# Queries' first block and the last block of rows at the matrix engine's full width, with half of x copied

## The chip, the cores and the metric

The kernel runs on one core of a Trainium2 chip. The core has a matrix engine (TensorE; PE in the profile, its weight loads PEld), VectorE (DVE), ScalarE (ACT), GpSimd (POOL) and DMA queues that SyncE (SP) issues. They run side by side, each through its own list of instructions in order, and wait for one another by semaphores. The metric is the device time of one execution in microseconds.

## The reference

Block-causal attention over 576 positions (8 batches, 8 heads, head size 64), and a mixer on its output:

```python
scores = scale * np.matmul(q, k.transpose(0, 1, 3, 2))
scores = np.where(block_i >= block_j, scores, -1e9)      # blocks of 64 positions
attn = softmax(scores)
x = matmul(attn, v)                                       # heads side by side: (8, 576, 512)
theta = x @ w_theta
y = w_tok_r @ (x * cos(theta)) + w_tok_i @ (x * sin(theta))
u = x + y
out = u + maximum(u @ w_ch, 0)
```

## The kernel before

Every product is done in float16 parts: an operand is a high part and a low part, and three matmuls (high by high, low by high, high by low) make one product. Heads come in pairs (`Pair`, 32 of them; head `hh` = 0 or 1 of a pair holds partitions 0 to 63 or 64 to 127 of the q and k tiles). Positions stand in the order 64 to 575 and then 0 to 63, so each head has four tiles of 128 queries, `i` = 3, 2, 1, 0, and a last half tile `i` = 4, which is the first 64 queries.

For one pair these steps run. `q_high`, `k_high` (POOL) and `q_low`, `k_low` (DVE) cut q and k in parts. `scores_wide` and `scores_narrow` multiply them on PE with 64 rows of the array per head, two heads beside each other (lines 552 and 558). `scores_first` (line 580) does the first 64 queries of both heads in quarters of the array, 64 by 64: three products by two heads, six matmuls. `maxima` and `less` (DVE, lines 597 and 602), `exponentials` and `high` (ACT, 607 and 618) and `low` (DVE, 622) make the attention parts, and a DMA transposes them (`turn`). `weighted` (line 645) multiplies them with v on PE, into one bank of PSUM, `o`, that all heads share. Of a head's 15 blocks the last, `i` = 4, holds both heads' first 64 queries; each head takes its 64 columns of the block as weights, and writes them twice, to partitions 0 to 63 and 64 to 127, since the mixer reads the half tile of x from both halves. That is six matmuls with 64 columns of weights behind 42 with 128. `normalise` (DVE) is three instructions: add a small number, take the reciprocal `r`, and multiply `o` by it into `xn` (lines 651, 653 and 657).

The mixer of a batch then turns x (759, 762, 765), multiplies by w_theta (773), takes sines and cosines (780 to 799), multiplies by x on POOL (808), cuts z in parts (817, 822), does the token mix (838, 831), and the channel product (856) with its closing steps (842 to 865).

The order of the work is a table. The kernel lists 3437 steps with what each needs; `ORDER` gives the sequence in which they are emitted, and so the list of each engine, and `BANKS` gives the PSUM banks. Steps of several pairs and batches are interleaved. The first matmuls of a step carry its waits.

Of the kernel before, what the change touches and what calls it, by code (L numbers as in the profile page):

```python
# [14 lines left out]
F16 = mybir.dt.float16  # L15
BF16 = mybir.dt.bfloat16
I32 = mybir.dt.int32
U32 = mybir.dt.uint32
AF = mybir.ActivationFunctionType
ALU = mybir.AluOpType  # L20
# [8 lines left out]
QK_BUFS = 2  # L29
# [208 lines left out]


@with_exitstack  # L240
def attention_phase_mixer(
    ctx: ExitStack,
    tc: tile.TileContext,
    qk: bass.AP,
    v: bass.AP,
    w_theta: bass.AP,
    w_tok: bass.AP,
    w_ch: bass.AP,
    out: bass.AP,
):  # L250
# [857 lines left out]
```

## Time and profile before

| | us |
|---|---|
| median of 3 runs | 728.31 (726.88 to 729.43) |
| profiled execution: span | 723.6 |
| what the median has beyond that span | 4.7 |
| PE busy | 640.6 (89%) |
| DVE busy | 588.8 (81%) |
| ACT busy | 589.0 (81%) |
| POOL busy | 270.9 (37%) |

The shares of busy time are means over stages: a start with the weights' preparation, a long stretch in which attention of one batch runs beside the mixers of others, and an end with mixers alone. A matmul's row gives its latency, and many are under way at once, so the cost of a matmul on PE is read from start to start.

### The profile page before, as it was taken

The numbers are of one execution on the slowest core, as the hardware profiler recorded it, in microseconds if no ns is written. First come the engines' busy times: TensorE is split into PE (matmuls) and PEld (weight loads), VectorE is DVE, ScalarE is ACT, GpSimd is POOL, SyncE is SP. The second block draws the span as 40 slices with busy tenths as digits, with TensorE's granted clock in tenths as the row PEclk, the third lists the DMA queues.
The fourth block names the chain that finished last, engine by engine and source line by source line (L and its number), as shares of the span: only waits on it lengthen the run. The fifth ranks groups of instructions, "written<-read, shape, count | busy, mean of one in ns | idle before, by whom it ended". The sixth has DMA issues, their size and how long they took to land.

```text
span 723.6 us, 19051 instructions
## 1 busy us (share of the span) xinstructions
PE 640.6 (89%) x7899; PEld 462.0 (64%) x7899; DVE 588.8 (81%) x1157; ACT 589.0 (81%) x900; POOL 270.9 (37%) x328
## 2 busy tenths in 40 slices
PE   0236489689999999999999999999999999999997
PEld 0124355566577767776667866777577577867776
DVE  6999999999888877888899879888888889642423
ACT  4899989999899789977999789969998899447231
POOL 3121120765155417441356302760083351412620
PEclk9656689899999999999999999999999999999999
DMA  8899999698768785784889994879879719840001
GB/s 297 306 252 195 204 145 192 172 169 159 141 187 175 141 181 152 150 194 90 178 194 198 176 184 119 176 181 154 185 177 183 144 31 157 168 73 17 34 34 66
DMA packets 263399, 114.54 MB, mean 158 GB/s; under 512 B 250896, under 2 KB 250896, under 8 KB 263312
## 3 DMA queue, kind: packets, MB, share of 16 engines
q1 hardware_dynamic: 263312, 113.33, 72.2%
q8 instruction: 61, 1.00, 0.6%
q14 instruction: 26, 0.21, 0.1%
HBM read 40.96 MB, written 9.44 MB: 70 GB/s over the span
## 4 chain that ended last, share of the span: by engine, by line
PE 52%; DVE 21%; ACT 17%; issue 6%; DMA 3%; POOL 0%; DVEq 0%; ACTq 0%; SPq 0%
PE g L838 13%; PE g L645 7%; PE s L838 7%; PE s L773 5%; DVE m L597 5%; PE g L856 4%; DVE p L622 4%; ACT t L607 4%; PE g L773 4%; PE s L856 4%; PE s L552 3%; ACT p L618 2%; PE g L552 2%; DVE rr L785 1%; DMA w_raw<-in_w_tok 1%
## 5 line engine op out<-in xcount | busy, mean ns | idle before, releaser
L622 DVE SCALAR_TENSOR_TENSOR p<-t,p 128x1600 f16<-128x1600 f32 (+3 forms) x80 | 121.8, 1525 | 18.6 <-ACT p L618 18.3
L838 PEld LDWEIGHTS <-zh 128*128 128x128 f16 x1152 | 112.8, 98 | 31.6 <-issue 0.2
L645 PE MATMUL g<-v,pt 128*128 128x65 f16 (+1 forms) x3072 | 112.1, 198 | 18.5 <-DMA pt<-p 8.3
L645 PEld LDWEIGHTS <-pt 128*128 128x128 f16 (+1 forms) x3072 | 105.7, 101 | 30.5 <-issue 12.0
L838 PE MATMUL g<-wT_h,zl 128*128 128x288 f16 x414 | 118.8, 287 | 1.3 <-DVE zl L822 1.0
L838 PE MATMUL g<-wT_h,zh 128*128 128x288 f16 x414 | 119.2, 288 | 0.5 <-DVE rr L785 0.3
L838 PE MATMUL g<-wT_l,zh 128*128 128x288 f16 x414 | 118.7, 287 | 0.0
L607 ACT ACTIVATE t<-s,m,size 128x576 f32<-128x576 f32 (+1 forms) x128 | 97.8, 777 | 17.7 <-DVE m L602 12.1
L808 POOL TENSOR_TENSOR aa<-aa,xn 128x256 f32<-128x256 f32 (+1 forms) x96 | 79.6, 847 | 63.0 <-ACT aa L797 43.4
L618 ACT ACTIVATE p<-t 128x1600 f16<-128x1600 f32 (+3 forms) x80 | 99.6, 1252 | 1.3 <-DMA pt<-p 0.3
L597 DVE TENSOR_REDUCE m<-s 128x1 f32<-128x576 f32 (+1 forms) x128 | 84.6, 680 | 4.6 <-PE s L558 4.1
L607 ACT ACTIVATE t<-g,m,size 128x320 f32<-128x320 f32 (+2 forms) x160 | 80.5, 532 | 3.9 <-DVE m L602 2.8
L773 PEld LDWEIGHTS <-xT 128*128 128x128 f16 x480 | 46.1, 98 | 51.2 <-issue 0.5
L808 POOL TENSOR_TENSOR rr<-rr,xn 128x256 f32<-128x256 f32 x64 | 59.0, 936 | 46.5 <-ACT rr L799 46.5
L838 PEld LDWEIGHTS <-zl 128*128 128x128 f16 x576 | 56.5, 98 | 19.7 <-issue 2.5
L552 PEld LDWEIGHTS <-qh 64*128 64x128 f16 x896 | 37.0, 98 | 45.0 <-issue 18.4
L597 DVE TENSOR_REDUCE m<-g 128x1 f32<-128x320 f32 (+2 forms) x160 | 56.5, 374 | 4.3 <-PE g L558 2.1
L856 PEld LDWEIGHTS <-wch_h 128*128 128x128 f16 x512 | 47.8, 98 | 17.4 <-issue 3.8
L822 POOL TENSOR_TENSOR zl<-rr,zh 128x512 f16<-128x512 f32 x32 | 41.1, 1287 | 37.7 <-ACT zh L817 31.5
L518 POOL TENSOR_SCALAR qh<-rq,size 128x576 f16<-128x576 f32 x32 | 28.7, 898 | 65.2 <-PE g L558 45.3
L849 DVE SCALAR_TENSOR_TENSOR ul<-u,size_ch,uh 128x576 f16<-128x576 f32 x32 | 28.0, 886 | 26.8 <-ACT uh L845 26.8
L773 PE MATMUL g<-wth_h,xT 128*128 128x512 f16 x160 | 47.6, 379 | 0.1
(152 smaller groups left out, 1552.2 us busy)
## 6 DMA issues: line engine op xcount, KB each, us to landing
rv<-in_v SPq DMA_DIRECT2D x16, 768.0 KB, 5.2
rq<-in_qk SPq DMA_DIRECT2D x16, 576.0 KB, 4.8
rk<-in_qk SPq DMA_DIRECT2D x16, 576.0 KB, 4.8
out<-u SPq DMA_DIRECT2D x32, 288.0 KB, 2.8
w_raw<-in_w_tok SPq DMA_DIRECT2D x9, 576.0 KB, 4.8
w_raw<-in_w_theta SPq DMA_DIRECT2D x4, 512.0 KB, 5.5
w_raw<-in_w_ch SPq DMA_DIRECT2D x4, 512.0 KB, 4.1
pt<-p SPq DMA_TRANSPOSE x80, 5.8
```

What stands on the lines that cost most here:

```text
L518: nc.gpsimd.tensor_scalar(out=self.qh, in0=self.raw("q"), scalar1=self.of.ups[0], scalar2=0.0, op0=ALU.mult, op1=ALU.add)
L552: nc.tensor.matmul(to[hh][:, col:col + n], lhsT=qq[rows, 64 + P * i:64 + P * i + P], rhs=kk[rows, k0:k0 + n], start=nn == 0 and col % 512 ...
L597: nc.vector.tensor_reduce(out=self.m[:, i:i + 1], in_=self.scores_of(i), axis=AX.X, op=ALU.max)
L607: nc.scalar.activation(out=t_parts[self.hh][:, to:to + n], in_=self.scores_of(i), func=AF.Exp, scale=self.pair.of.scale, bias=self.m[:, NI ...
L618: nc.scalar.mul(hi, x, LIFT)
L622: nc.vector.scalar_tensor_tensor(out=lo, in0=x, scalar=LIFT, in1=hi, op0=ALU.mult, op1=ALU.subtract)
L645: nc.tensor.matmul(o[to, i, :], lhsT=pp, rhs=vv[:, slot, hh, :], start=first, stop=last)
L773: nc.tensor.matmul(g, lhsT=xT[:, dt, xx + i, :], rhs=ww[:, dt, :], start=dt == 0 and n == 0, stop=dt == NDT - 1 and n == 2)
L808: nc.gpsimd.tensor_tensor(out=cd, in0=cd, in1=self.xns[dt][:, i0:i0 + ni, :], op=ALU.mult)
L822: engine.tensor_tensor(out=zl, in0=cv, in1=zh, op=ALU.subtract)
L838: nc.tensor.matmul(g, lhsT=zz[:, kk, cols], rhs=ww[:, kk, ts], start=(n == 0 and kk == k0 and nn == 0), stop=False)
L856: nc.tensor.matmul(g[:, 0:HS], lhsT=ww[:, dt, e * P:(e + 1) * P], rhs=uu[:, dt, th * HS:(th + 1) * HS], start=dt == 0 and n == 0, stop=dt ...
```

## The change

`scores_first` becomes three matmuls over the whole array. For that the host lays q out with 64 more columns: the first 128 columns hold the first 64 queries of head 0 (on partitions 0 to 63, zeros below) and then those of head 1 (on partitions 64 to 127, zeros above), so that one matmul with 128 rows gives both heads. The q tiles and their parts are therefore 640 wide instead of 576.

`weighted` treats the last block as the others: three matmuls with 128 columns of weights. The half of `o` that belongs to the other head holds nothing of use for this head, and a new DVE instruction in `normalise` multiplies the right 64 rows of `o` by `r` once more and writes them to the other 64 partitions of `xn`.

`junk`, which only receives the absolute values of a sum on ACT, has one byte an element. `ORDER` and `BANKS` are found anew.

```diff
 ORDER = [
-    24, 25, 26, 27, 28, 29, 0, 173, 8, 177, 16, 1, 2, 3, 174, 9, 4, 10, 32, 11, 178, 12, 56, 185, 17, 186, 33, 18,
...
 BANKS = (
...
-    junk = const.tile([P, PG * NI * P], BF16, name="junk")
+    junk = const.tile([P, PG * NI * P], U8, name="junk")
...
-            return ld.tile([P, S], F16, tag=tag, name=tag, bufs=QK_BUFS)
+            return ld.tile([P, S + D if tag[0] == "q" else S], F16, tag=tag, name=tag, bufs=QK_BUFS)
...
-                            nc.tensor.matmul(to[hh][:, col:col + n], lhsT=qq[rows, 64 + P * i:64 + P * i + P], rhs=kk[rows, k0:k0 + n],
+                            nc.tensor.matmul(to[hh][:, col:col + n], lhsT=qq[rows, P + P * i:P + P * i + P], rhs=kk[rows, k0:k0 + n],
...
         def scores_first(self):
             for nn, qq, kk in self.products():
-                for hh in range(2):
-                    rows = slice(hh * D, hh * D + D)
-                    nc.tensor.matmul(self.first[rows], lhsT=qq[rows, 0:64], rhs=kk[rows, 0:64], start=nn == 0, stop=nn == 2,
-                                     tile_position=(hh * D, hh * D))
+                nc.tensor.matmul(self.first, lhsT=qq[:, 0:P], rhs=kk[:, 0:64], start=nn == 0, stop=nn == 2)
...
-                        pp, rows = source[:, block, :], [slice(0, P)]
-                        if i == 4:
-                            pp, rows = pp[:, 64 * hh:64 * hh + 64], [slice(0, 64), slice(64, P)]
-                        for to in rows:
-                            nc.tensor.matmul(o[to, i, :], lhsT=pp, rhs=vv[:, slot, hh, :], start=first, stop=last)
+                        nc.tensor.matmul(o[:, i, :], lhsT=source[:, block, :], rhs=vv[:, slot, hh, :], start=first, stop=last)
...
                                         in1=self.r.unsqueeze(2).broadcast_to([P, NI, D]), op=ALU.mult)
+                mine, other = (slice(x * D, x * D + D) for x in (hh, 1 - hh))
+                nc.vector.tensor_tensor(out=m.xns[pair.pr][other, NI - 1, mine], in0=o[mine, NI - 1, 0:D],
+                                        in1=self.r[mine, NI - 1:NI].broadcast_to([D, D]), op=ALU.mult)
...
+    q_first = np.zeros((B, G, P, PG, P), q.dtype)
+    for rows in (slice(0, D), slice(D, P)):
+        q_first[:, :, rows, :, rows] = q[:, :, rows, :, 0:D]
```

On PE, the first scores of pair 19 (`qh`, `ql` and `kh`, `kl` are the parts of q and k, `g_112` the bank that `o` and the first scores share) stand between two products of the channel step in both kernels. Before:

```order
L580 LDWEIGHTS qh
L580 MATMUL g_112<-kh,qh 64x64
L580 LDWEIGHTS qh
L580 MATMUL g_112<-kh,qh 64x64
L580 LDWEIGHTS ql
L580 MATMUL g_112<-kh,ql 64x64
L580 LDWEIGHTS ql
L580 MATMUL g_112<-kh,ql 64x64
L580 LDWEIGHTS qh
L580 MATMUL g_112<-kl,qh 64x64
L580 LDWEIGHTS qh
L580 MATMUL g_112<-kl,qh 64x64
```

and now:

```order
L853 MATMUL g_110<-uh,wch_l 128x288
L579 LDWEIGHTS qh
L579 MATMUL g_112<-kh,qh 128x64
L579 LDWEIGHTS ql
L579 MATMUL g_112<-kh,ql 128x64
L579 LDWEIGHTS qh
L579 MATMUL g_112<-kl,qh 128x64
L853 LDWEIGHTS wch_h
```

Six matmuls of a quarter of the array became three of the whole.

The end of a head's weighted sum on PE (head 30; `pt` is the transposed attention, `v` the parts of v, `zh` a part of the mixer's z). Before:

```order
L645 MATMUL g_112<-v_85,pt_104 128x65
L645 LDWEIGHTS pt_104
L645 MATMUL g_112<-v_85,pt_104 64x65
L645 LDWEIGHTS pt_104
L645 MATMUL g_112<-v_85,pt_104 64x65
L645 LDWEIGHTS pt_104
L645 MATMUL g_112<-v_86,pt_104 64x65
L645 LDWEIGHTS pt_104
L645 MATMUL g_112<-v_86,pt_104 64x65
L645 LDWEIGHTS pt_104
L645 MATMUL g_112<-v_85,pt_104 64x65
L838 LDWEIGHTS zh
```

and now:

```order
L639 LDWEIGHTS pt_104
L639 MATMUL g_112<-v_85,pt_104 128x65
L639 LDWEIGHTS pt_104
L639 MATMUL g_112<-v_86,pt_104 128x65
L639 LDWEIGHTS pt_104
L639 MATMUL g_112<-v_85,pt_104 128x65
L835 LDWEIGHTS zh
```

The half-width matmuls are gone, and three at full width close the head.

On DVE, the closing of head 31 with its waits (`r` is the reciprocal, `xn` the x of the pair). Before:

```order
L651 TENSOR_SCALAR r<-g_112 128x5 [waits PE_49]
L653 RECIPROCAL r<-r 128x5 [waits DVE_49]
L657 TENSOR_TENSOR xn<-g_112,r 128x5x64 [waits DVE_49,Activation_49]
L526 SCALAR_TENSOR_TENSOR ql<-rq,size,qh 128x576 [waits Pool_49]
L762 TENSOR_TENSOR xp<-xn,xp 128x640 [waits DMAHW0_49,Activation_49]
```

and now:

```order
L645 TENSOR_SCALAR r<-g_112 128x5 [waits PE_49]
L647 RECIPROCAL r<-r 128x5 [waits DVE_49]
L651 TENSOR_TENSOR xn<-g_112,r 128x5x64 [waits DVE_49]
L654 TENSOR_TENSOR xn<-g_112,r 64x64 [waits DVE_49]
L846 SCALAR_TENSOR_TENSOR ul<-u_4694,size_ch,uh 128x576 [waits Activation_49]
L759 TENSOR_TENSOR xp<-xn,xp 128x640 [waits DMAHW1_49,Activation_49]
```

The new instruction stands behind the multiplication, and waits for it on its own engine; what follows differs by the new table.

## Rows read from the trace of the kernel before

**Rows 1.** The page: the span, and each engine's busy time (share), instructions.
```profile
span 723.6 us, 19051 instructions
PE 640.6 (89%) x7899; PEld 462.0 (64%) x7899; DVE 588.8 (81%) x1157; ACT 589.0 (81%) x900; POOL 270.9 (37%) x328
```

**Rows 2.** Busy time by stage; the header names the columns.
```profile
core 0: us, PE busy (x) PEld busy (x) DVE busy (x) ACT busy (x) POOL busy (x), PEclk, DMA share, GB/s
0.00:165.00 165.00, 93.16 (x1349) 64.29 (x1350) 152.85 (x343) 146.67 (x248) 50.61 (x82) 0.80 0.92 215
165.00:590.00 425.00, 418.52 (x5287) 299.73 (x5286) 369.73 (x699) 377.31 (x552) 179.24 (x202) 1.00 0.77 163
590.00:620.00 30.00, 29.48 (x374) 22.47 (x372) 27.96 (x47) 26.76 (x42) 12.63 (x15) 1.00 0.70 122
620.00:723.60 103.60, 99.42 (x900) 75.54 (x895) 38.22 (x71) 38.21 (x61) 28.43 (x32) 1.00 0.24 61
```

**Rows 3.** DVE's longest waits, 165 to 620 us: total us, times, longest.
```profile
DVE p L622 <- ACT p L618: 16.2, 14, 3.4
DVE rr L785 <- ACT aa L780: 8.4, 11, 1.9
DVE r L651 <- PE g L645: 6.6, 8, 1.9
```

**Rows 4.** PE in order of time, a weighted sum's end: start, us, count.
```profile
332.53 0.41 PE L645 MATMUL g<-v,pt 128*128 128x65 f16 x7
...
332.65 0.28 PE L645 MATMUL g<-v,pt 128*64 128x65 f16 x6
332.87 0.30 PE L838 MATMUL g<-wT_h,zh 128*128 128x288 f16 x1
```

**Rows 5.** The same weighted sum, whole.
```profile
331.30 1.64 PE L645 MATMUL g<-v,pt 128*128 128x65 f16 x48
```

**Rows 6.** PE in order of time, first scores between two channel products.
```profile
370.44 0.29 PE L856 MATMUL g<-ul,wch_h 128*128 128x288 f16 x1
370.56 0.29 PE L856 MATMUL g<-uh,wch_l 128*128 128x288 f16 x1
370.77 0.22 PE L580 MATMUL g<-kh,qh 64*64 64x64 f16 x2
370.83 0.20 PE L580 MATMUL g<-kh,ql 64*64 64x64 f16 x2
370.86 0.20 PE L580 MATMUL g<-kl,qh 64*64 64x64 f16 x2
370.99 0.30 PE L856 MATMUL g<-uh,wch_h 128*128 128x288 f16 x1
```

**Rows 7.** PE in order of time, two ends of the other scores.
```profile
330.40 0.22 PE L558 MATMUL g<-ones,mask_q 64*128 64x128 bf16 x1
330.55 0.30 PE L838 MATMUL g<-wT_h,zh 128*128 128x288 f16 x1
...
350.20 0.22 PE L558 MATMUL s<-ones,mask_q 64*128 64x128 bf16 x2
350.35 0.22 PE L580 MATMUL g<-kh,qh 64*64 64x64 f16 x2
...
350.56 0.30 PE L838 MATMUL g<-wT_h,zh 128*128 128x288 f16 x1
```

**Rows 8.** DVE, ACT and POOL groups by shape: busy us, mean ns, idle before.
```profile
L657 DVE TENSOR_TENSOR xn<-g,r 128x320 f32<-128x320 f32 x64 | 31.1, 486 | 3.1 <-ACT t L607 1.6 <-DVE r L653 0.5
L651 DVE TENSOR_SCALAR r<-g 128x5 f32<-128x5 f32 x64 | 10.0, 157 | 15.8 <-PE g L645 14.1 <-ACT t L607 1.6
L597 DVE TENSOR_REDUCE m<-g 128x1 f32<-128x64 f32 x32 | 6.9, 216 | 2.1 <-ACT t L607 2.0
L822 DVE TENSOR_TENSOR zl<-aa,zh 128x256 f16<-128x256 f32 x16 | 8.3, 517 | 0.3 <-ACT zh L817 0.3
L526 DVE SCALAR_TENSOR_TENSOR ql<-rq,size,qh 128x576 f16<-128x576 f32 x32 | 28.4, 887 | 2.4 <-POOL qh L518 2.4
L737 ACT ACTIVATE junk<-rv 128x1280 bf16<-128x1280 f32 x16 | 20.3, 1269 | 1.4 <-DMA rv<-in_v 1.3
L737 ACT ACTIVATE junk<-rq 128x1152 bf16<-128x1152 f32 x16 | 18.6, 1164 | 0.1
L518 POOL TENSOR_SCALAR qh<-rq,size 128x576 f16<-128x576 f32 x32 | 28.7, 898 | 65.2 <-PE g L558 45.3 <-issue 9.1 <-PE g L580 5.2
```

**Rows 9.** DVE in order of time, a head's closing.
```profile
333.18 0.19 DVE L653 RECIPROCAL r<-r 128x5 f32<-128x5 f32 x1
333.40 0.49 DVE L657 TENSOR_TENSOR xn<-g,r 128x320 f32<-128x320 f32 x1
```

**Rows 10.** Line 552 until 162 us, and PE in order of time behind it.
```profile
L552 PE MATMUL s<-kh,qh x64: 187/290/605, 16.5 to 144.0; 64*128 64x64 f16 x32, 64*128 64x512 f16 x16, 64*128 64x384 f16 x16
...
162.18 0.42 PE L552 MATMUL s<-kh,qh 64*128 64x512 f16 x4
...
590.82 0.42 PE L552 MATMUL s<-kh,qh 64*128 64x512 f16 x4 [0.18 <-ACT t L607]
```

More of the change, by code (lines that the diff above doesn't have):

```diff
@@ L18 @@
 U32 = mybir.dt.uint32
+U8 = mybir.dt.uint8
 AF = mybir.ActivationFunctionType
@@ L34 @@
 ORDER = [
[178 rows of a table removed]
[177 rows of a table added]
 ]
 BANKS = (
-    "6555046500302240123540123640123560123540123540123650123640123540123540123460123540123560123560123460123650123460"
-    "1234601234501234601234601235401235601236401234501236401235401236401235401234501234501236401236454260645665611660"
-    "6425451201054465450410201125045446566640505146450620154064566154055530410416604565165504145605061546650064161165"
-    "405623065434601256253044530560235465102"
+    "5611645600406140123640123450123540123560123450123260123450123540123460123640123560123540123650123450123450123450"
+    "1234601235401236401234601236401236401234601236501236401235601235401236401235401234601235601235465041645646540542"
+    "4644450611056626564606101216046464556601505565643051450055654055155520640654604516565606056426150445541251045065"
+    "416036452636046151143624532652053461502"
 )
@@ L243, in attention_phase_mixer @@
     tc: tile.TileContext,
-    qk: bass.AP,
+    q: bass.AP,
+    k: bass.AP,
     v: bass.AP,
@@ L251, in attention_phase_mixer @@
     nc = tc.nc
-    B, _, NG, P, PG, S = qk.shape
+    B, NG, P, PG, S = k.shape
     D = P // 2
@@ L728, in load @@
             self.scales_of(what, g).make()
-            shape, src = ([P, PG, NV, 2, D], v[self.b, g]) if what == "v" else ([P, PG, S], qk[self.b, "qk".index(what), g])
+            shape, src = ([P, PG, NV, 2, D], v[self.b, g]) if what == "v" else ([P, PG, (S, S + D)[what == "q"]], (k, q)[what == "q"][self.b, g])
             self.raw[what, g] = ld.tile(shape, F32, tag=f"r{what}{g}", name=f"r{what}")
@@ L1083 @@
     v_pad[:, :, :, :, 1:5] = v[..., 64:S, :].reshape(B, G, PG, 2, 4, P, D)
+    q, k = (a.reshape(B, G, PG, 2, S, D).transpose(0, 1, 3, 5, 2, 4).reshape(B, G, P, PG, S) for a in (q, k))
+    q_first = np.zeros((B, G, P, PG, P), q.dtype)
+    for rows in (slice(0, D), slice(D, P)):
+        q_first[:, :, rows, :, rows] = q[:, :, rows, :, 0:D]
     laid = {
-        "qk": np.stack([a.reshape(B, G, PG, 2, S, D).transpose(0, 1, 3, 5, 2, 4).reshape(B, G, P, PG, S) for a in (q, k)], axis=1),
+        "q": np.concatenate([q_first, q[..., D:]], axis=-1),
+        "k": k,
         "v": v_pad.transpose(0, 1, 5, 2, 4, 3, 6),
```

354 rows, old and new, of the table ORDER are left out of this document.

## The prediction

> **What bounds the kernel now.** I read the page's busy times first [rows 1]: PE 640.6 us of 723.6, DVE and ACT 81% each. That mean hides three stages, so the busy times by stretch came next [rows 2]. In the first 165 us DVE is busy 152.85 us and PE only 93.16: this start is bound by DVE, with ACT close by. From 165 to 590 us PE is busy 418.52 of 425 us (98.5%), DVE 87%, ACT 89%: PE bounds, but two engines are near. After 620 us DVE and ACT are under 40% and PE is at 96%. Third, the waits from 165 to 620 us [rows 3]: DVE's longest are for ACT's high part (16.2 us), then for ACT's rounding (8.4) and for the weighted sum (6.6), so DVE's idle time is partly spent in a chain with ACT, not only because PE is late. Last, PE in order of time, start to start, since a matmul's own duration is latency.
>
> **What the change removes on PE.** In a weighted sum the last full-width matmul starts at 332.53, the first of half width at 332.65, and the next step at 332.87 [rows 4]. The 42 full ones start between 331.30 [rows 5] and 332.53, 1.23 us over 41 steps, or 0.03 us each. So the six of half width cost 332.87 - 332.56 = 0.31 us, most of it on going in and coming out. Three of full width cost 3 x 0.03 = 0.09. Saved: 0.22 us a head, 14.1 us for 64 heads.
>
> First scores between two full-width steps: the matmul before them starts at 370.56, a 288-column one takes 0.12 (370.44 to 370.56), so the next could start at 370.68; it starts at 370.99 [rows 6]. The six cost 0.31 us, three at 0.03 cost 0.09 (the nearest row: 65 columns against full weights): 0.22 saved. Behind the other scores the way back to full width costs 0.15 alone (330.40 to 330.55), and with first scores between 0.36 (350.20 to 350.56) [rows 7]: the six cost 0.21, saved 0.12. Between two steps of the other scores, three at full width need their own way in (those 0.15) and a way back to half rows, which I estimate at the 0.09 that the way into quarters takes (0.21 from 370.56 to 370.77, less the 0.12); of the six's 0.36 little is left to save, 0.03. The orders have mostly the first two kinds; I take 0.17, bounds 0.03 and 0.22: 32 x 0.17 = 5.4 us, bounds 1.0 and 7.0.
>
> Only what lies where PE bounds counts. Eight pairs' wide scores (16 matmuls of 512 columns) lie ahead of 162 us, so the group at 162.18 is pair 8's [rows 10], and the start ends there. Ahead of it both orders have 14 closed heads. That leaves 50 heads x 0.22 = 11.0 and 24 pairs x 0.17 = 4.1: **15.1 us off the path** (11.7 to 16.3).
>
> For pricing small tiles the Trainium skill has another rule (TensorE: Matmul & The Clock Gate, part 3 on packing small matmuls): tiles in different rows and columns of the array run concurrently, so two quarter-array matmuls take about the time of one. The trace agrees that they start in pairs [rows 6], but not that the group is as cheap as three full ones: 0.31 us against 0.09. By that rule alone PE would gain nothing, which is the last rival below.
>
> **What it adds on DVE.** 64 new instructions, 64 by 64, PSUM to SBUF. No row has this form. Between 157 ns for 5 columns and 486 for 320 [rows 8] a line gives 219 ns at 64 columns; the reduction over 64 columns out of PSUM takes 216. I take 0.22. Bounds: 0.157, and 0.317 (the row with two tensors out of SBUF, 517 ns at 256 columns, brought to 64 by that line's 1.04 ns a column). The copy waits for the instruction before it, on its own engine. Such a pair is seen at 333.18: 0.19 long, the dependent one starts at 333.40, so 0.03 after the end [rows 9]. Each copy thus costs 0.25 us of DVE (0.19 to 0.35), 16.0 us in all. `ql` grows from 576 to 640 columns: in proportion 887 x 64/576 = 0.10 us [rows 8], 32 times, 3.2 us (from 0, if the 64 columns are free).
>
> The copy also keeps the bank `o` 0.25 us longer. The next head's weighted sum waits for it, and PE holds what stands behind that sum; but from 165 us on some 8.5 us pass per head (425 us for 50), against about 1.6 for a sum [rows 5] and 1.2 for its closing with the copy, so the order has room, and I count nothing; uncovered it would be 50 x 0.25 = 12.5 us.
>
> In the start, DVE bounds: 14 copies and 8 `ql` are 3.5 + 0.8 = **4.3 us on the path** (0 if the new order puts off other DVE work; 7 if steps of later heads come ahead as well).
>
> From 165 to 590 us DVE gets 46 copies and 22 `ql`, 11.5 + 2.2 = 13.7 us, while the stretch should shrink by about 13. It would be busy 383 of 412 us, 93% instead of 87%. What that does to PE no row of this stretch shows. It is 0 if all of DVE's 55 idle us can shrink: from 590 to 620 us DVE is busy 27.96 of 30, also 93%, and PE still 29.48 [rows 2]. It is 13.7 if none can, since each added microsecond then delays the scores' maxima and low parts by which PE is fed. As about half of the waits in rows 3 are on ACT, which is at 89% and gains no speed, I take **4 us**, nearer to the row that shows 93%.
>
> **What lies beside.** ACT's sum over q grows by 128 columns, (1269 - 1164) = 0.105 us, 16 times, 1.7 us; POOL's `qh` by at most 898 x 64/576 = 0.10 us, 32 times, at 37% busy [rows 1, 8]. ACT has 48 us idle in the long stretch, and both are covered there; uncovered ACT's part costs 1.7. The bytes of `junk` are written, not read: nothing. q's DMAs carry a ninth more, 16 times; they are issued a batch ahead, and the DMA engines are at 0.77 of their time [rows 2]. In the start, at 0.92, it may cost up to 1 us, inside the bound above. The new tables keep the makeup: pair, head and mixer steps stand in nearly the same counts ahead of the same places, and I give their reshuffling no gain or loss of its own.
>
> **Sum.** -15.1 + 4.3 + 4 = -6.8 us on the profiled execution: span 716.8. The runs' median is 4.7 us above that span, and the change touches nothing outside it: **721.5 us**.
>
> **Rivals.**
> 1. *Everything added is hidden.* For it: DVE has 55 idle us in the long stretch and the table was found with the copy in it. Against it: DVE's 12 idle us in the start are short waits. Time: -15.1, 713.2; at the upper price of the first scores 712.
> 2. *DVE becomes the bound* (the other side). Its place is the long stretch, the price 13.7 us, and it decides once DVE's waits for ACT do not shrink, for DVE and ACT would both be over 92% and feed each other through the maxima, exponentials, high and low parts. -15.1 + 4.3 + 13.7 = +2.9: 731.2. With half of the waits shrinking, 724.3. Against it: the 93% of 590 to 620 us with PE busy.
> 3. *The tiles were as cheap as full width*: PE gains nothing, and 4.3 + 4 us stay, so 736.6. For it speaks only the pairs' common start; rows 4, 6 and 7 speak against it.
>
> **How the numbers follow.** Forecast 0.52, with its own range 717 to 726.5; rival 1 0.17; rival 2 0.27, spread from 726 to 734; rival 3 0.04. Below 0.3%, about 2.2 us, a measurement of this kernel can't be told from no change. Faster by more than that is under 726.1: 0.49 of the forecast and all of rival 1, 0.66. Slower is over 730.5: 0.14 of rival 2 and rival 3, 0.18. The rest, 0.16, is no change. The range that holds 8 in 10 is 712 to 732: it cuts rival 1's and rival 2's far ends and leaves out rival 3.
>
> **What would show it.** PE: 192 fewer matmuls in the weighted sums and 96 in the first scores; a head's 45 start 0.03 us apart to the end, and the next step 0.03 us after the last; three first scores take 0.09 to 0.1 us beside full-width steps; PE's busy time falls by some 18 us. DVE: 64 rows of the copy at about 220 ns, each 0.03 us behind its predecessor; busy up by about 17 us. The stretch up to pair 8's scores ends 4 us later, near 166 us, and the one to pair 30's scores, now from 162.18 to 590.82 [rows 10], takes about 419 us instead of 428.6. I am wrong if PE's idle time past 165 us grows by more than 10 us with DVE or ACT as what it waits for (rival 2), if the start grows by far more than 4 us, or if the matmuls at full width come farther than 0.05 us apart.

## The result, and the profile after

The changed kernel takes 739.09 us (median; 737.19 to 740.55) against 728.09 for the kernel before in the same comparison: a ratio of 1.0145 (95% interval 1.0124 to 1.0166). It is slower by some 11 us, where 721.5 was predicted and 732 was the end of the range. The page of the changed kernel, whose columns are those of [rows 1]:

```profile
span 738.8 us, 18542 instructions
PE 621.7 (84%) x7611; PEld 453.1 (61%) x7611; DVE 615.9 (83%) x1221; ACT 591.2 (80%) x900; POOL 271.9 (37%) x328
```

PE has 288 matmuls fewer, as foreseen, and 18.9 us less busy time, where some 18 were foreseen; DVE's busy time grew by 27.1 us, where 17 were. The marks of the stages (pair 8's and pair 30's first wide scores) in PE's order of time, which answer to [rows 10]:

```profile
174.43 0.42 PE L553 MATMUL s<-kh,qh 64*128 64x512 f16 x4
...
610.05 0.48 PE L553 MATMUL s<-kh,qh 64*128 64x512 f16 x3
```

Cut at these marks, busy time by stage, with the columns of [rows 2]. After:

```profile
0.00:174.43 174.43, 87.79 (x1252) 61.95 (x1254) 157.02 (x358) 146.93 (x243) 48.94 (x82) 0.91 0.84 201
174.43:610.05 435.62, 410.25 (x5140) 296.20 (x5140) 391.40 (x743) 383.09 (x563) 180.60 (x202) 1.00 0.76 162
610.05:738.80 128.75, 123.66 (x1221) 94.94 (x1220) 67.45 (x122) 61.14 (x97) 42.36 (x45) 0.99 0.35 77
```

and the kernel before at its own marks:

```profile
0.00:162.18 162.18, 91.19 (x1316) 63.17 (x1316) 150.03 (x339) 143.85 (x244) 49.39 (x81) 0.80 0.92 216
162.18:590.82 428.64, 421.13 (x5323) 301.22 (x5323) 373.37 (x704) 380.95 (x559) 181.28 (x202) 1.00 0.77 162
590.82:723.60 132.78, 128.26 (x1261) 97.64 (x1260) 65.37 (x116) 64.15 (x100) 40.24 (x46) 1.00 0.35 75
```

The start grew by 12.2 us, the long stretch by 7.0, and the tail shrank by 4.0. In the stretch PE was busy 10.9 us less, and still the stretch took longer: what it does not work rose from 7.5 to 25.4 us, while DVE's busy time rose by 18.0 and DVE's idle time fell from 55.3 to 44.2.

These profiles are 15.2 us apart and the medians 11.0. The profiled run of the changed kernel took 740.55 us, the slowest of its four. The span of 723.6 before is a fast execution: 44 later runs of that kernel have spans of 723.9 to 728.3. So a stage's difference of 3 us between two profiles says little; the verdicts below rest on medians.

What PE saves at each place came as the steps priced it. A head's weighted sum (answering to [rows 5]) and first scores between two channel products (to [rows 6]):

```profile
340.40 1.53 PE L639 MATMUL g<-v,pt 128*128 128x65 f16 x45
...
384.89 0.29 PE L853 MATMUL g<-uh,wch_l 128*128 128x288 f16 x1
385.02 0.19 PE L579 MATMUL g<-kh,qh 128*128 128x64 f16 x1
385.05 0.19 PE L579 MATMUL g<-kh,ql 128*128 128x64 f16 x1
385.07 0.19 PE L579 MATMUL g<-kl,qh 128*128 128x64 f16 x1
385.10 0.29 PE L853 MATMUL g<-uh,wch_h 128*128 128x288 f16 x1
```

Less the 0.20 of the last matmul's own latency, 45 matmuls take 1.33 us over 44 steps, 0.03 apart to the end. The three first scores take 385.10 - 385.02 = 0.08 us to the next channel product; by the prediction's counting (385.10 - 384.89, less 0.12 for the product ahead) it is 0.09, where six took 0.31.

The groups by shape that answer to [rows 8] (busy us, mean ns, idle before):

```profile
L519 POOL TENSOR_SCALAR qh<-rq,size 128x640 f16<-128x640 f32 x32 | 38.1, 1190 | 48.0 <-PE g L559 22.5 <-PE s L559 16.4 <-issue 5.4
L527 DVE SCALAR_TENSOR_TENSOR ql<-rq,size,qh 128x640 f16<-128x640 f32 x32 | 29.9, 934 | 0.1
L734 ACT ACTIVATE junk<-rq 128x1280 uint8<-128x1280 f32 x16 | 20.3, 1269 | 1.0 <-DMA rq<-in_q 1.0
L654 DVE TENSOR_TENSOR xn<-g,r 64x64 f32<-64x64 f32 x64 | 14.2, 222 | 2.2
```

The copy itself takes 222 ns, as estimated. But 64 of them are 14.2 us and `ql` grew by 1.5, while DVE is busy 27.1 us more: something else on DVE cost more too. DVE's longest waits in the stretch (us, times, longest):

```profile
DVE p L620 <- ACT p L616: 8.7, 11, 1.9
DVE r L645 <- PE g L639: 7.3, 6, 2.9
DVE rr L782 <- ACT aa L777: 6.5, 11, 1.6
```

Those for ACT's high part fell from 16.2 [rows 3] to 8.7, about half, and the wait for PE hardly moved. PE's longest from 165 to 605 us, after:

```profile
PE g L639 <- DMA pt<-p: 6.7, 8, 1.6
PE g L853 <- ACT t L605: 1.6, 2, 1.2
```

and before:

```profile
PE s L856 <- ACT t L607: 1.2, 3, 0.5
PE g L856 <- DVE u L861: 1.0, 1, 1.0
```

PE now waits longest for the transposed attention, the last link of the chain from the maxima (DVE) over exponentials and high part (ACT) and low part (DVE) to the transposing DMA. All of PE's waits in these 440 us add up to 25.7 us, where they were 6.3: 9.3 of them for DVE, 9.2 for DMAs and 5.3 for ACT.

### The profile page after: what moved, and what is told of

Read it like the earlier page. It is cut to its first block, busy times and chain, and to the rows that moved or that the text cites. A ratio compares the mean times of both kernels' runs of the same rounds, so it can differ in the third digit from the quotient of the medians.

```text
span 738.8 us, 18542 instructions
## 1 busy us (share of the span) xinstructions
PE 621.7 (84%) x7611; PEld 453.1 (61%) x7611; DVE 615.9 (83%) x1221; ACT 591.2 (80%) x900; POOL 271.9 (37%) x328
## 4 chain that ended last, share of the span: by engine, by line
PE 36%; DMA 8%; ACT 5%; DVE 5%; issue 2%; POOL 1%; ACTq 0%; DVEq 0%; POOLq 0%
PE g L835 11%; DMA pt<-p 6%; PE s L835 5%; PE g L639 4%; PE g L853 4%; PE s L770 3%; PE s L853 3%; PE g L770 3%; DMA xT<-xp 2%; ACT t L605 1%; DVE m L595 1%; PE s L553 1%; PE g L828 1%; PE g L553 1%; DMA out<-u 1%
## 5 line engine op out<-in xcount | busy, mean ns | idle before, releaser
L639 PE MATMUL g<-v,pt 128*128 128x65 f16 x2880 | 105.2, 198 | 34.5 <-DMA pt<-p 16.4
L639 PEld LDWEIGHTS <-pt 128*128 128x128 f16 x2880 | 100.6, 100 | 44.7 <-DMA pt<-p 22.2
L620 DVE SCALAR_TENSOR_TENSOR p<-t,p 128x1600 f16<-128x1600 f32 (+4 forms) x80 | 118.6, 1489 | 9.8 <-ACT p L616 9.6
L605 ACT ACTIVATE t<-s,m,size 128x576 f32<-128x576 f32 (+2 forms) x130 | 97.7, 773 | 13.8 <-DVE m L600 9.8
L616 ACT ACTIVATE p<-t 128x1600 f16<-128x1600 f32 (+4 forms) x80 | 99.7, 1251 | 3.2 <-DMA pt<-p 2.1
L605 ACT ACTIVATE t<-g,m,size 128x192 f32<-128x192 f32 (+2 forms) x158 | 79.9, 531 | 11.9 <-DVE m L600 7.6
L595 DVE TENSOR_REDUCE m<-s 128x1 f32<-128x448 f32 (+2 forms) x130 | 85.3, 676 | 2.2 <-PE s L559 1.6
L595 DVE TENSOR_REDUCE m<-g 128x1 f32<-128x192 f32 (+2 forms) x158 | 55.7, 371 | 5.2 <-PE g L559 2.8
L523 POOL TENSOR_SCALAR kh<-rk,size 128x576 f16<-128x576 f32 x32 | 30.6, 958 | 77.4 <-PE g L559 26.3
L519 POOL TENSOR_SCALAR qh<-rq,size 128x640 f16<-128x640 f32 x32 | 38.1, 1190 | 48.0 <-PE g L559 22.5
```

The source lines that it names most:

```text
L519: nc.gpsimd.tensor_scalar(out=self.qh, in0=self.raw("q"), scalar1=self.of.ups[0], scalar2=0.0, op0=ALU.mult, op1=ALU.add)
L595: nc.vector.tensor_reduce(out=self.m[:, i:i + 1], in_=self.scores_of(i), axis=AX.X, op=ALU.max)
L605: nc.scalar.activation(out=t_parts[self.hh][:, to:to + n], in_=self.scores_of(i), func=AF.Exp, scale=self.pair.of.scale, bias=self.m[:, NI ...
L616: nc.scalar.mul(hi, x, LIFT)
L620: nc.vector.scalar_tensor_tensor(out=lo, in0=x, scalar=LIFT, in1=hi, op0=ALU.mult, op1=ALU.subtract)
L639: nc.tensor.matmul(o[:, i, :], lhsT=source[:, block, :], rhs=vv[:, slot, hh, :], start=first, stop=last)
```

## The experiments

Theory P (the prediction's): PE is the bound, what it saves is time won, and the copies cost little. Theory D: DVE is the pace, and PE's saving is worth nothing. Theory T: the new tables cost the time. Theory J came later: under an order made for one balance of the engines, PE, DVE and ACT are tied, so that load on any of them comes through and relief of one gives nothing. "Old tables" are `ORDER` and `BANKS` of the kernel before. Busy times are those of the profiles' pages.

### Code and tables apart

The first run is the changed code with the old tables, the second the old code with the new ones.

```diff
-ORDER, BANKS: new        (e1: changed code)
+ORDER, BANKS: old
-ORDER, BANKS: old        (e2: old code)
+ORDER, BANKS: new
```

> All code edits of the change, with the ORDER and BANKS of the kernel before. Theory T (the new tables feed PE worse, the edits themselves are worth what was forecast): about 721 us, clearly under 728.1, and the start up to pair 8's scores ends near 166 us. Theory D (the 64 copies on DVE hold up PE whatever the order): 735 to 742, as the change, with the start again near 174 us. In between, 726 to 732: both.

> The code of the kernel before with the new ORDER and BANKS. Theory T: slower than before by as much as the tables cost, 736 us or more (the 15 us that PE gained are missing, so up to 745). Theory D: no copies, so near 728 to 731.

Measured: 741.53 us for the edits with old tables, ratio 1.0184 (1.0165 to 1.0203); 737.13 for the old code with new tables, 1.0124 (1.0107 to 1.0142). The first met D's forecast, the second T's and not D's. So the edits alone cost all of the loss and more, and the new tables win back some 2.4 us for the code they were found for (the two intervals just touch), at a price of 9 for the old one. The stages of the two, start and stretch; e1:

```profile
0.00:169.29 169.29, 92.07 (x1250) 63.13 (x1251) 156.03 (x353) 146.33 (x244) 47.56 (x81) 0.84 0.85 210
169.29:609.48 440.19, 415.54 (x5122) 296.91 (x5122) 392.12 (x748) 381.62 (x557) 177.72 (x202) 1.00 0.75 159
```

e2:

```profile
0.00:166.86 166.86, 87.32 (x1318) 61.51 (x1319) 153.31 (x345) 147.28 (x246) 48.12 (x82) 0.83 0.89 208
166.86:603.46 436.60, 421.18 (x5338) 303.29 (x5337) 378.30 (x698) 381.05 (x560) 183.97 (x202) 1.00 0.77 160
```

The start's 12.2 us come as 7.1 from the edits (169.29) and 4.7 from the tables (166.86 in e2 without any edit). In the stretch the edits cost 11.6, and the new tables bring this down to 7.0. Each of these is read off one profile. Theory T is not the loss, though the tables seem to be part of the start.

PE's busy time does not follow the edits alone: it fell by 6.1 us with all edits and old tables (634.5 in e1), by 6.6 with the new tables and no edit (634.0 in e2), and by 18.9 with both.

### The two edits apart

```diff
 # e3: first scores, q's layout and junk as changed; weighted and normalise as before; old tables
+                nc.tensor.matmul(self.first, lhsT=qq[:, 0:P], rhs=kk[:, 0:64], start=nn == 0, stop=nn == 2)
 # e4: the rest as before; old tables
+                        nc.tensor.matmul(o[:, i, :], lhsT=source[:, block, :], rhs=vv[:, slot, hh, :], start=first, stop=last)
+                nc.vector.tensor_tensor(out=m.xns[pair.pr][other, NI - 1, mine], in0=o[mine, NI - 1, 0:D],
+                                        in1=self.r[mine, NI - 1:NI].broadcast_to([D, D]), op=ALU.mult)
```

> Only the first scores by block-diagonal q (q 640 wide), old tables; weighted sums as before and no copy. Both theories: PE gains 4 us past the start, DVE and ACT get about 1.5 us each of wider q: 724 to 727.

> Only the weighted sums at full width and the copies on DVE, old tables; first scores as before. Theory T: -11 us on PE, +3.5 in the start, up to +4 behind it: 721 to 726. Theory D: the copies' 16 us come through: 732 or more.

Measured: first scores alone 731.63, ratio 1.0043 (1.0030 to 1.0057): slower, where either theory had them faster. The wider q must cost more than PE's few microseconds give; whether by DVE, ACT, POOL or the transfers was not separated. Weighted sum with copy 742.25, 1.0185 (1.0165 to 1.0205): the whole loss of the edits. PE's longest wait from 165 to 605 us in e4 is one on ACT's exponentials, which free banks:

```profile
PE s L837 <- ACT t L607: 6.2, 6, 2.6
```

It was 0.9 us in the kernel before (line 838 there). ACT's own longest wait is one step further back, on DVE's `less`; e4:

```profile
ACT t L607 <- DVE m L602: 19.1, 20, 4.7
```

and before, over the same 165 to 605 us:

```profile
ACT t L607 <- DVE m L602: 8.9, 13, 2.3
```

The copies delay the next head's maxima and `less`, these ACT, and ACT frees PE's banks later. But the copies are not all of it. In e5 below, which has no copy, PE already waits

```profile
PE s L834 <- ACT t L607: 4.4, 6, 1.7
```

presumably because a PE with less to do comes to the same wait earlier. ACT's wait for `less` is 12.0 us there, and 16.5 in e6, which has the copies alone. The copy's hold on the bank `o` shows too: PE's weighted sums wait 3.0 us for it in e4.

### PE's saving and DVE's copies apart

```diff
 # e5: as e4, without the copy
-                nc.vector.tensor_tensor(out=m.xns[pair.pr][other, NI - 1, mine], ...
 # e6: kernel before, with the copy alone (six half-width matmuls kept)
+                nc.vector.tensor_tensor(out=m.xns[pair.pr][other, NI - 1, mine], ...
```

> Weighted sums at full width and no copy at all (half of the last tile of x is left wrong), old tables: PE's 11 us past the start are given back with nothing added on DVE. Theory P (PE bounds the long stretch, as forecast): 715 to 719, the stretch from pair 8's to pair 30's scores 418 us instead of 428.6. Theory D (the stretch is set by the chain of DVE and ACT, and PE's idle time merely looks small): 726 to 729, the stretch 427 to 429 and PE idle 10 us more. Both tight at once: 721 to 724.

> The kernel before with the 64 copies added on DVE and nothing else (they write what is there already), old tables. Theory P: up to 4 us in the start and some of the 55 idle us of DVE used, 732 to 736. Theory D: each copy's 0.25 us comes through, start 3.5 and stretch 11.7: 742 to 745, as with the weighted sums changed (742.3) although PE's work is 14 us more.

Measured: PE's saving with nothing added 724.58, ratio 0.9953 (0.9935 to 0.9970), nearest to the case in which both are tight; the copies with nothing saved 741.80, 1.0200 (1.0172 to 1.0228), just under D's range. The stretch of e5:

```profile
165.10:592.91 427.81, 413.75 (x5191) 295.85 (x5191) 376.28 (x703) 379.81 (x558) 181.59 (x202) 1.00 0.78 163
```

PE works 7.4 us less there than before and the stretch is 0.8 shorter, where P had 10.6. The saving of 64 x 0.22 = 14.1 us gives 3.4 in the median. This fells P's main step. With the copies in, it gives nothing that can be told from zero (e4 742.25 against e6 741.80). The copies alone cost 14.6, where the forecast counted 3.5 in the start and less than 4 in the stretch. The chain that ended last, followed back over the whole span, lay on PE for only half of it already in the kernel before:

```profile
PE 52%; DVE 21%; ACT 17%; issue 6%; DMA 3%; POOL 0%; DVEq 0%; ACTq 0%; SPq 0%
```

and the copies alone move it to DVE (e6):

```profile
PE 47%; DVE 34%; ACT 10%; issue 6%; DMA 3%; POOL 0%; DVEq 0%; ACTq 0%; SPq 0%
```

The busy times of e6 show how much DVE gets:

```profile
PE 645.9 (87%) x7899; PEld 464.8 (63%) x7899; DVE 611.2 (83%) x1221; ACT 590.1 (80%) x900; POOL 261.6 (35%) x328
```

DVE is busy 22.4 us more, 0.35 a copy, though a copy lasts 0.22. Of this 14.1 us are the copies themselves, 3.1 are other instructions that lasted longer, and 5.2 are time in which two instructions overlapped before and no longer do. DVE in order of time in e6:

```profile
339.37 0.49 DVE L657 TENSOR_TENSOR xn<-g,r 128x320 f32<-128x320 f32 x1
339.89 0.23 DVE L660 TENSOR_TENSOR xn<-g,r 64x64 f32<-64x64 f32 x1
340.15 0.17 DVE L375 TENSOR_SCALAR size<-size 128x3 int32<-128x3 int32 x1
340.35 0.76 DVE L597 TENSOR_REDUCE m<-s 128x1 f32<-128x576 f32 x1
341.03 0.21 DVE L597 TENSOR_REDUCE m<-g 128x1 f32<-128x64 f32 x1
341.16 0.51 DVE L868 TENSOR_SCALAR u<-u,size 128x576 f32<-128x576 f32 x1
```

Independent instructions overlap: 341.03 begins 0.08 before the end of the one at 340.35, and 341.16 begins 0.08 before 341.24. The copy begins 0.03 after the multiplication it waits for, and the next 0.03 after the copy. From the multiplication's end at 339.86 to the next start are 0.29 us; where the next had begun 0.08 early, the copy costs 0.37. Over all 64 copies of e6 both gaps are 0.03 us in the median, and in the kernel before 51 of the 64 multiplications are followed by an instruction that begins 0.08 before their end. Why the instruction behind the copy, which needs nothing of it, begins no earlier stays open.

### Where the copy is made

```diff
 # e7: as e5, and on POOL
+                nc.gpsimd.tensor_copy(out=m.xns[pair.pr][other, NI - 1, mine], in_=m.xns[pair.pr][mine, NI - 1, mine])
 # e8: as e5, and on DVE, out of SBUF
+                nc.vector.tensor_copy(out=m.xns[pair.pr][other, NI - 1, mine], in_=m.xns[pair.pr][mine, NI - 1, mine])
 # e16: as e5, and on DVE, out of SBUF, both halves at the head of the step that cuts x (x_high)
+                nc.vector.tensor_copy(out=self.xns[dt][other, NI - 1, mine], in_=self.xns[dt][mine, NI - 1, mine])
```

> Weighted sums at full width, and the copy taken by POOL out of xn (SBUF to SBUF, behind the head's multiplication) instead of DVE out of PSUM, old tables. Theory P: 716 to 722. Theory D: DVE has no more work than before, so 726 to 730; over 733 if POOL's list, which waits for DVE at each copy, then holds back qh, kh and the products by x.

> As the weighted sums with copy, but DVE copies out of xn (SBUF, no second tensor) instead of multiplying out of PSUM. It still waits for the multiplication before it. If the copy takes 0.15 us instead of 0.22, theory D: 64 x 0.07 = 4.5 us less than 742.3, 737 to 739. Theory P: no difference beyond 2 us from 742.3.

> Weighted sums at full width, and DVE's copies out of xn (SBUF, 0.31 us) put off to the place ahead of ACT's high part of x, behind both heads: the same DVE work as in the variant with copies out of SBUF (741.8), but no copy stands at a head's closing, where the next weighted sum waits for the bank and where it waits for the multiplication before it. If the place of the copy matters: 733 to 738. If DVE's time alone matters: 740 to 743.

Measured: on POOL 732.93, ratio 1.0078 (1.0058 to 1.0097); on DVE out of SBUF 741.76, 1.0202 (1.0181 to 1.0223), as out of PSUM; late, 756.78, 1.0400 (1.0374 to 1.0426). Out of SBUF the copy no longer holds the bank `o`, but it lasts 0.09 us longer, so the bank cannot be more than a few microseconds of the price. The copy's own rows by shape in e7,

```profile
L656 POOL COPY xn<-xn 64x64 f32<-64x64 f32 x64 | 32.5, 508 | 150.7 <-DVE xn L653 114.5 <-DVE size L700 15.7 <-DVE m L602 12.7
```

and in e8:

```profile
L656 DVE COPY xn<-xn 64x64 f32<-64x64 f32 x64 | 19.7, 308 | 2.2
```

POOL, at 37% busy, takes the copies off DVE, and then 9 us less are lost. It is still slower than before, and 8.4 us slower than e5, with DVE no busier than before (589.4 us): DVE's time is not the copy's whole price. What of the rest is POOL's list and what x being complete later was not tried. The late copies cost twice the early ones for the same 64 copies on DVE; the place matters, but the other way than was expected. ACT's longest wait in e16:

```profile
ACT xp L757 <- DVE xn L756: 50.6, 26, 9.3
```

It was 18.2 us in the kernel before for the same instruction of ACT. At the head of the step the copies stand directly ahead of ACT's cast of x, behind whatever else DVE has in its list, and ACT stands still for it.

### Relief on DVE

The guard that DVE adds to the sums (1e-9 by scale) is left out: one instruction less a head. The version without it, of the kernel before (e9), of e4 (e10), of the changed kernel (e11), of e5 (e12):

```diff
-                nc.vector.tensor_scalar(out=self.r, in0=o[:, :, D], scalar1=1.0e-9 * LIFT, scalar2=None, op0=ALU.add)
+                nc.vector.reciprocal(out=self.r, in_=o[:, :, D])
...
-                nc.vector.reciprocal(out=self.r, in_=self.r)
+                pass
```

> The kernel before without the addition ahead of the reciprocal (the reciprocal reads PSUM; the number added is under half a unit in the last place of the sums, which hold at least one full weight). DVE loses 64 instructions of 0.157 us, 35 of them with a dependent one right behind: some 0.14 us a head, 2 in the start, 6.4 in the stretch. Theory D (DVE sets start and stretch): 719 to 722. Theory P (PE sets the stretch): 725 to 728, the stretch 427 to 429.

> Weighted sums at full width with DVE's copy, old tables, without the addition. DVE has 0.25 - 0.14 = 0.11 us a head more than before. Theory D: 742.3 - 9 = 732 to 735, still slower than before although PE has 14 us less. Theory P: 716 to 724.

> The whole change with its own tables, without the addition. Theory D: 739.1 - 9 = 729 to 732. Theory P: 737 to 739.

> Weighted sums at full width, no copy (half of x's last tile is left wrong) and no addition, old tables: both PE and DVE relieved. Theory D: DVE's 9 us come off 724.6, 715 to 718; it is below e9 by as much as PE still counts, 2 to 5 us. Theory P: no lower than 722.

Measured: e9 725.09, ratio 0.9971 (0.9961 to 0.9982), the fastest here that computes all of the output, ahead of both kernels; e10 736.77, 1.0137 (1.0115 to 1.0158), 0.0048 under e4; e11 736.36, 1.0119 (1.0092 to 1.0147), 0.0026 under the changed kernel, within the two intervals; e12 721.13, 0.9919 (0.9898 to 0.9940). The stretch in e9:

```profile
160.61:588.96 428.35, 420.60 (x5323) 301.21 (x5323) 368.90 (x660) 380.49 (x559) 179.79 (x202) 1.00 0.77 163
```

and in e12:

```profile
163.28:588.24 424.96, 413.62 (x5192) 295.59 (x5191) 369.56 (x659) 379.57 (x557) 178.33 (x202) 1.00 0.78 164
```

D in its plain form falls here: none of its four forecasts held, and 4.5 us off DVE in the stretch shorten it by 0.3. P's held for e9 alone. With PE relieved as well the stretch is 3.7 shorter, more than the two apart (0.8 and 0.3) together, but such differences are within what single profiles vary by. In the medians the two about add up (3.4 and 2.1 against 5.9).

### Load on each engine alone

```diff
 # e13: PE: the half-width block multiplied three times over, 12 matmuls more a head
+                    for nn, (block, vv) in (3 if i == 4 else 1) * list(enumerate(((high, pair.v1), (high, pair.v2), (low, pair.v1)))):
 # e14: ACT: a cast of 128 by 128 that nobody waits for, one a head
+                nc.scalar.copy(out=junk[:, 0:P], in_=ident)
 # e15: DVE: the copy of e6 for the first head of a pair only
+                if hh == 0:
```

> The kernel before with only PE loaded: the last block's six half-width matmuls are issued three times (the same result), 12 more a head, some 0.2 us, 13 us in all, 9 in the stretch. Theory D (DVE and ACT set the stretch, PE follows): at most 3 us more, 727 to 731. Theory J (the table holds PE and DVE's chain tied, so that relief of one gives nothing and load on either comes through): 734 to 739, the stretch 436 to 439.

> The kernel before with only ACT loaded: 64 copies of a constant, 128 columns, no wait in front, about 0.2 us of ACT each behind the overlap, 13 us in all. Theory D: through the exponentials it comes through, 734 to 742. Theory J: the same. Theory DVE-alone (only DVE is tied): 728 to 731.

> The kernel before with the copies of head 0 of each pair alone, 32 instead of 64. If DVE has no slack at all: half of 14 us, 733 to 736. If some slack is used up first: less than a third, 728 to 732.

Measured: PE 734.31, ratio 1.0094 (1.0072 to 1.0115); ACT 735.92, 1.0109 (1.0084 to 1.0133); half the copies 732.47, 1.0069 (1.0043 to 1.0095). The loads on PE and ACT came in J's range, and half the copies between its two cases. The pages, e13:

```profile
PE 653.6 (89%) x8667; PEld 475.7 (65%) x8667; DVE 589.8 (81%) x1157; ACT 589.9 (81%) x900; POOL 266.7 (36%) x328
```

e14:

```profile
PE 642.4 (88%) x7899; PEld 463.5 (63%) x7899; DVE 592.8 (81%) x1157; ACT 601.2 (82%) x964; POOL 268.3 (37%) x328
```

e15:

```profile
PE 643.0 (88%) x7899; PEld 463.1 (63%) x7899; DVE 598.9 (82%) x1189; ACT 589.9 (81%) x900; POOL 269.8 (37%) x328
```

All doses together, as change in the engine's busy time, change in the median (ratio less 1, times 728.3), and the share of the one in the other, with the bounds that the ratio's interval gives:

| on | run | busy us | time us | share |
|---|---|---|---|---|
| PE | e5 | -9.1 | -3.4 | 0.4 (0.2 to 0.5) |
| PE | e13 | +13.0 | +6.8 | 0.5 (0.4 to 0.65) |
| ACT | e14 | +12.2 | +7.9 | 0.65 (0.5 to 0.8) |
| DVE | e9 | -6.7 | -2.1 | 0.3 (0.2 to 0.4) |
| DVE | e15 | +10.1 | +5.0 | 0.5 (0.3 to 0.7) |
| DVE | e6 | +22.4 | +14.6 | 0.65 (0.55 to 0.75) |
| DVE, with the copies | e10 against e4 | -8.0 | -3.5 | 0.4 (0.2 to 0.7) |
| PE, with the copies | e4 against e6 | -10.1 | -1.1, intervals overlap | 0 to 0.4 |

(e5's PE busy time is 631.5, e9's DVE 582.1, e4's PE 635.8; DVE is at 613.4 in e4 and 605.4 in e10; the others stand on the pages above.) The busy times are rough as well: DVE's rose by 4.3 us in e5 and PE's by 5.3 in e6 with no edit to their work. And e13's matmuls close a weighted sum for which DVE's closing waits, so they load that chain too. No engine is the pace alone, and none of the three is free. Reliefs tend to give less than loads cost, but most bounds meet, so that is not shown. J's half on loads held; by the other half relief of one should give nothing, and it gave 2.1 and 3.4 us. That it is the fixed order that ties the engines was not tried, as no order was found anew for e5 or e9, nor a second one for the changed code.

## Why the prediction was wrong, point by point

- **PE's saving per instruction** was right: 0.03 us a matmul to the end of a weighted sum, and 0.09 for three first scores. That PE's busy time fell by 18.9 us against some 18 is in part luck: with the old tables the same edits took off 6.1 (e1).
- **"15.1 us off the path" failed, and it is the largest error.** It was read from PE busy 418.52 of 425 us [rows 2]. e5 shows what that saving is worth with nothing added: 3.4 us. A high share of busy time, with two engines at 87% and 89% in the same stretch and one order for all three, was no proof of a sole bound; the chain that ended last had PE in 52% of the span. The Trainium skill warns of that reading (Perfetto Trace Analysis, Identifying the Most-Contended Engine): matmul busy time is not a good measure, because matmuls are pipelined, and TensorE's headroom is to be judged by its weight loads (and by its arithmetic). By the weight loads PE stood at 299.73 of 425 us, 71%, under ACT and DVE [rows 2], and e5 agrees. e13 does not agree that PE had slack, since half of a load on it came through.
- **The copy on DVE**: its duration was right (222 ns against 0.22 us), its price was not: 0.37 us of DVE's order where 0.25 was counted and 0.35 was the upper bound. The prediction counted the copy's length and the gap ahead of it; it left out the gap behind and the overlap of 0.08 us that the neighbours lose.
- **"I take 4 us" for the copies in the stretch failed.** It leaned on the 30 us of [rows 2] in which DVE is 93% busy and PE still works, and on "about half" of the waits in [rows 3] being on ACT; they are 24.6 us of 31.2, over three quarters. The share of DVE's load that comes through is 0.5 to 0.65 (e15, e6), not 0.3, and in e6 the stretch grew by 9.0 us (437.65 against 428.64).
- **The start** was to grow by 4.3 and grew by 12.2. Of this the edits made 7.1 (e1), near the upper bound of 7, and the tables 4.7 (e2), each by one profile. **"No gain or loss" for the tables** was thus wrong in the start; over the whole program they bring some 2.4 us with the new code.
- **What lies beside**: `ql` grew by 0.05 us (0.10 was counted) and ACT's sum by the 0.105 counted. Yet with the wider q the first scores, priced at 5.4 us saved on PE, were a loss of 3.2 us (e3), with DVE busy 5.3 us more and ACT 1.9.
- **The 4.7 us between span and median** are not all time outside the program: single runs took 1.7 to 3.2 us more than their own spans, and the rest is that the profiled execution was a fast one. In the changed kernel's profile the difference was 0.3. This did no harm, since by medians alone the forecast's -6.8 stands against +11.0.
- **Rival 2** was nearest. Its sign came: past 165 us PE idles more by over 10 us (7.5 to 25.4 in the stretch), most of it for DVE, ACT and what they feed. Its condition, that DVE's waits for ACT do not shrink, was not met: the longest fell from 16.2 to 8.7, for which it had 724.3. Its price was too low even at 731.2, because it still took off PE's 15.1. Its own terms without that credit, 4.3 + 13.7, are 18.0; the measured 11.0 lies below, with a part of PE's saving and the new tables in it. Rivals 1 and 3 fell (e6; the matmuls' rows).

Open: whether relief truly gives less than load costs, and whether the fixed order is the reason; and e5's start, which was 165.1 us in its profile against 162.2 with less work in it.

## What to carry to other kernels

Work taken from one engine and put on another may be summed only with a share for each, and the shares are had by dosing: a harmless extra instruction on each engine in turn tells what a microsecond there costs before anything is moved. Where three engines run at 87 to 98% under one written order, expect neither a saving on one of them in full nor a load on another for free: here 0.5 to 0.65 of a load came through and 0.3 to 0.4 of a relief, with wide bounds. Price an added instruction that waits for the one before it with the gaps on both sides and the overlap that its neighbours lose, not by its length alone.

## What the runs showed of the hardware

POOL's `qh` took 1190 ns in the changed kernel, 0.29 more than before, where 0.10 was the bound. It isn't the width: with the old tables the 640 columns take 962 (e3), and with the new tables 576 columns take 1186 (e2). Its median is 0.80 us in the changed kernel, and 11 of the 32 took over 1 us. POOL in order of time in the changed kernel (start, us):

```profile
338.31 2.58 POOL L519 TENSOR_SCALAR qh<-rq,size 128x640 f16<-128x640 f32 x1
...
341.60 0.79 POOL L519 TENSOR_SCALAR qh<-rq,size 128x640 f16<-128x640 f32 x1
```

and DVE in the same stretch:

```profile
338.57 1.74 DVE L620 SCALAR_TENSOR_TENSOR p<-t,p 128x1536 f16<-128x1536 f32 x1
```

The long one, 2.58 us, encloses DVE's `low`, which reads two tensors out of SBUF, as if it stood still for those 1.74 us. The Trainium skill (GPSIMD Engine Reference, Specifications) says that POOL shares its SBUF interfaces with VectorE and contends with instructions there that have two SBUF inputs; these rows agree. What this cost the whole was not tried.

On DVE, 64 by 64 values to the other partitions took 222 ns as a multiplication out of PSUM and 308 as a plain copy out of SBUF (e8); on POOL the copy took 508 (e7).
